# Attention into a Mish layer: tile 0's q as f32 on SyncE's queue, cast by three engines, and w_in issued ahead of v's casts

## The chip, the cores and the metric

The kernel runs on one core of one Trainium2 chip. The metric is the device time of one execution in microseconds (us); a time quoted for a kernel is the median of several runs. A core has five engines with a queue of instructions each: TensorE (PE, with its weight loads PEld), VectorE (DVE), ScalarE (ACT), GpSimd (POOL) and SyncE (SP). Each runs its queue in order and waits on semaphores for the others. Transfers (DMA) are issued from an engine's queue and move their bytes on 16 DMA engines.

## The reference

```
scores = q @ k^T / sqrt(64)                      # 8 batches, 8 heads, 576 positions, 64 wide
D[h]   = gamma_h ** (i - j) for i >= j, else 0   # gamma_h = 1 - 2 ** (-5 - h)
att    = (scores * D) @ v
x      = att, heads side by side                 # 4608 x 512
h      = x @ w_in                                # 512 x 2048
g      = h * tanh(softplus(h))                   # Mish
out    = g @ w_out                               # 2048 x 512
```

All inputs and the output are f32; the kernel multiplies in bf16.

## The kernel before

**Tiles.** The 4608 rows are cut into 36 chunks of 128 rows, and four chunks make a tile of 512 rows, so there are nine tiles. Tiles 0 and 1 hold the first 128 positions of each of the eight batches; they need no state of earlier positions and have a path of their own (functions whose names begin with `f_`). The other tiles carry a state matrix from chunk to chunk.

**The first layer** is `g1(t, f)` (L360): for one of 16 blocks `f` of 128 columns of w_in, four matmuls into `hp` and a Mish on ScalarE into `gT` (L367). For tile 0, blocks 0 to 3 are done in two halves of the columns, first for chunks 0 and 1 and then for chunks 2 and 3 (L456 to L461), blocks 4 to 15 whole (L487). The second layer follows with `g2_first`, `g2` and `g2_last`.

**The order of all work is written by hand** (`manual_schedule`): each engine runs its instructions in the order in which the program text names them. Waits come from the data.

**Tile 0's path.** `load_first_qk(t, i, b)` (L99) loads q (i = 0) or k (i = 1) of one batch, all heads, on GpSimd's queue; the transfer casts f32 to bf16 and its target is `stage`, the first of two buffers of `gT`. `load_first_v(b)` (L107) loads v of two batches as f32, also into `stage`. `f_transpose(t, g, i, parts)` (L175) transposes two batches (pair `g`) of q or k on TensorE and copies the result out of PSUM with the engines named in `parts`. `f_scores` (L198) makes the scores of a pair and multiplies them on VectorE by `dmask` (L208, two per pair). `f_v` (L213) casts v to bf16 with the engine that it is given, `f_out` (L218) multiplies scores and v and copies into `xT`, the input of `g1`. `keep_warm(n)` (L157) issues n matmuls on zeros, whose results are not used.

**GpSimd's queue at the start.** Loads of k and q of batches 0 and 1 (L117), `make_identity` for `ident` (needed by every transpose on TensorE, L125), `dist` (L126 to L130, from which VectorE makes `dmask` at L146), loads of k and q of batches 2 and 3 (L131), `pos`, v of batches 0 and 1, the first quarter of w_in (L139), v of batches 2 and 3. Then two casts of v (L447, L448), and only then the other three quarters of w_in (L449, L450), a third cast of v (L453), and the loads of tile 1 and w_out. The fourth cast of v is ScalarE's (L454), ahead of the first Mish in its queue. SyncE's queue issues the stores of the output and, late in the kernel, transposing transfers; it has nothing to issue in the first 50 us.

Of the kernel before, what the change touches and what calls it, by code (L numbers as in the profile page):

```python
# [10 lines left out]
F32 = mybir.dt.float32  # L11
BF16 = mybir.dt.bfloat16
AX = mybir.ActivationFunctionType
# [4 lines left out]
def kernel(  # L18
# [18 lines left out]
    nc = tc.nc  # L37
    B, H, S, D = q.shape
    assert (B, H, S, D) == (8, 8, 576, 64)
    P = 128  # L40
# [3 lines left out]
    nF = d_ff // P  # L44
    KC = d_model // P
    NCH = 4
# [15 lines left out]
    consts = ctx.enter_context(tc.tile_pool(name="consts", bufs=1))  # L62
# [6 lines left out]
    gp = ctx.enter_context(tc.tile_pool(name="gp", bufs=2))  # L69
    op = ctx.enter_context(tc.tile_pool(name="op", bufs=4))  # L70
    PS = bass.MemoryType.PSUM
    ps_sc = ctx.enter_context(tc.tile_pool(name="ps_sc", bufs=2, space=PS))
    ps_st = ctx.enter_context(tc.tile_pool(name="ps_st", bufs=1, space=PS))
# [11 lines left out]
    def load_w_in(f0, n):  # L85
        nc.gpsimd.dma_start(out=w_in_t[:, :, ds(f0, n)], in_=w_in_r[:, :, ds(f0, n)])
# [6 lines left out]


    stage = gp.tile([P, nF, NCH * P], BF16, name="gT")
    v0 = {}
    fst = {}

    def load_first_qk(t, i, b):  # L99

        name = ("qb", "kb")[i]
        if t not in fst:
            fst[t] = {"qb": stage[:, 0:4, :], "kb": stage[:, 4:8, :], "vb": {}}
        nc.gpsimd.dma_start(out=fst[t][name][:, b, :],  # L104
                            in_=(q, k)[i][4 * t + b, :, 0:P, :].rearrange("h (g r) d -> g h (r d)", r=8))

    def load_first_v(b):  # L107

        if b < 4:
            pair = stage[:, ds(8 + 2 * b, 4), :].bitcast(F32).rearrange("p a (c d) -> p (a c) d", d=D)  # L110
        else:
            pair = first.tile([P, 2 * H, D], F32, name="vpair", bufs=2)
        for e in range(2):
            v0[b + e] = pair[:, ds(H * e, H), :]
        nc.gpsimd.dma_start(out=pair, in_=v[ds(b, 2), :, 0:P, :].rearrange("b h p d -> p (b h) d"))

    for i, b in ((1, 0), (1, 1), (0, 0), (0, 1)):  # L117
        load_first_qk(0, i, b)

    zeros = consts.tile([P, 512], BF16)  # L120
    nc.vector.memset(zeros, 0.0)
    lnd = consts.tile([P, 1], F32)
    nc.vector.memset(lnd, -0.5 * math.log(D))
    ident = consts.tile([P, P], BF16)
    make_identity(nc, ident)  # L125
    dist = consts.tile([P, P], F32)  # L126
    nc.gpsimd.iota(dist, pattern=[[1, P]], base=0, channel_multiplier=-1,
                   allow_small_or_imprecise_dtypes=True)
    nc.gpsimd.affine_select(out=dist, in_=dist, compare_op=OP.is_ge, fill=1.0e6,
                            base=0, pattern=[[1, P]], channel_multiplier=-1)  # L130
    for i, b in ((1, 2), (1, 3), (0, 2), (0, 3)):  # L131
        load_first_qk(0, i, b)
    pos = consts.tile([P, 5], F32)
    nc.gpsimd.iota(pos, pattern=[[P, 5]], base=0, channel_multiplier=1,
                   allow_small_or_imprecise_dtypes=True)
# [2 lines left out]
    load_first_v(0)  # L138
    load_w_in(0, 512)  # L139
    load_first_v(2)  # L140
    mask = consts.tile([P, P], F32)
    mask2 = consts.tile([P, P], F32)
    lg = [math.log(1.0 - 2.0 ** (-5.0 - h)) for h in range(H)]
    dmask = consts.tile([P, H, P], F32)
# [12 lines left out]
    def keep_warm(n, pool=ps_o, name="ops"):  # L157
        idle = pool.tile([P, 512], F32, name=name)
        for _ in range(n):
            nc.tensor.matmul(idle, lhsT=zeros[:, 0:P], rhs=zeros, start=True, stop=True)  # L160
# [14 lines left out]
    def f_transpose(t, g, i, parts):  # L175

        name = ("qb", "kb")[i]
        out_t = first.tile([P, H, P], BF16, name=name + "T", bufs=2)
        n = 8 // len(parts)
        moves = []  # L180
        for j, (pool, tname, copy) in enumerate(parts):
            tp = pool.tile([P, 2, 8, P] if tname == "sc" else [P, 8, P], BF16, name=tname)
            tp = (tp[:, 0] if tname == "sc" else tp)[:, 0:n]
            for r in range(n):
                if t == 1:
                    mix = fst[1][name, "mix", g][:, n * j + r]
                    nc.tensor.transpose(tp[:, r, :], mix.rearrange("p x d -> p (x d)"), ident)
                else:
                    for x in range(2):
                        nc.tensor.transpose(tp[ds(64 * x, 64), r, :],  # L190
                                            fst[0][name][:, 2 * g + x, ts(n * j + r, D)], ident)
            moves.append((copy, out_t.rearrange("p h (g r) -> p h g r", r=8)[:, :, :, ds(n * j, n)],
                          tp.rearrange("p r (g h) -> p h g r", h=H)))
        for copy, to, src in moves:
            copy(to, src)
        fst[t][name, g] = out_t

    def f_scores(t, g, between=None):  # L198
        qT, kT = fst[t]["qb", g], fst[t]["kb", g]
        scs = [ps_sc.tile([P, 2, NP, P], F32, name="sc").rearrange("p a b i -> p (a b) i") for _ in range(2)]  # L200
        for h in range(H):
            for x in range(2):
                r = ds(64 * x, 64)
                nc.tensor.matmul(scs[x][:, h, :], lhsT=kT[r, h, :], rhs=qT[r, h, :], start=True, stop=True)  # L204
        for x in range(2):
            b = 2 * g + x
            sm = first.tile([P, H, P], BF16, name="sm0", bufs=4)
            nc.vector.tensor_tensor(sm, scs[x], dmask, op=OP.mult)  # L208
            fst[t]["sm", b] = sm
            if between and x == 0:  # L210
                between()

    def f_v(t, b, copy):  # L213
        vb = first.tile([P, H, D], BF16, name="vb", bufs=4)
        copy(vb, v0[4 * t + b])
        fst[t]["vb"][b] = vb

    def f_out(t, b, copy):  # L218
        if b == 0:
            xts[t] = xp.tile([P, KC, NCH * P], BF16, name="xT")  # L220
        vb = fst[t]["vb"][b]
        if t == 0:
            pool, name = ((ps_h, "hp"), (ps_h, "hp"), (ps_st, "st"), (ps_o, "ops"))[b]
            ot = pool.tile([P, NP, P], F32, name=name)
        else:
            ot = ps_sc.tile([P, 2, NP, P], F32, name="sc")[:, 0]
        for p in range(NP):
            for e in range(2):
                nc.tensor.matmul(ot[ds(64 * e, 64), p, :], lhsT=vb[:, 2 * p + e, :],
                                 rhs=fst[t]["sm", b][:, 2 * p + e, :],  # L230
                                 start=(p == 0), stop=True, skip_group_check=True)
        copy(xts[t][:, :, ts(b, P)], ot)
# [121 lines left out]
            xts[t] = xp.tile([P, KC, NCH * P], BF16, name="xT")  # L354
        nc.vector.tensor_copy(xts[t][:, :, ts(s, P)], ot)  # L355

    gts = {}
    outs = {}

    def g1(t, f, cols=slice(0, NCH * P)):  # L360
# [69 lines left out]
    dve, act, pool = nc.vector.tensor_copy, nc.scalar.copy, nc.gpsimd.tensor_copy  # L430


    half = (slice(0, 2 * P), slice(2 * P, 4 * P))
    keep_warm(7)
    f_transpose(0, 0, 1, [(ps_h, "hp", act), (ps_h, "hp", dve)])
    nc.scalar.activation(dmask, dmask, AX.Exp, bias=lnd[:, 0:1])
    f_transpose(0, 0, 0, [(ps_st, "st", act), (ps_o, "ops", dve)])
    for h in range(H):
        nc.vector.tensor_scalar(ex[:, :, h], pos, lg[h], None, op0=OP.mult)
    f_transpose(0, 1, 1, [(ps_h, "hp", act), (ps_h, "hp", act)])  # L440
    f_scores(0, 0)
    f_transpose(0, 1, 0, [(ps_st, "st", act), (ps_o, "ops", act)])
    keep_warm(4, ps_h, "hp")
    nc.scalar.activation(gq, ex, AX.Exp)
# [1 line left out]
    nc.scalar.activation(warm, lnd, AX.Mish)  # L446
    f_v(0, 0, pool)  # L447
    f_v(0, 1, pool)  # L448
    for i in range(1, 4):  # L449
        load_w_in(512 * i, 512)  # L450
    f_scores(0, 1, lambda: f_out(0, 0, dve))
    f_out(0, 1, act)
    f_v(0, 2, pool)  # L453
# [168 lines left out]
```

## Time and profile before

| | |
|---|---|
| runs | 317.28, 317.5, 318.41 us; median 317.5 |
| profiled execution | 319.16 us |
| its span, first to last instruction | 317.5 us |
| mean granted TensorE clock | 0.988 |
| TensorE busy | 302.5 us (95%) |
| VectorE, ScalarE, GpSimd busy | 133.2, 111.2, 144.7 us |
| GpSimd's transfer queue | 27.80 MB |
| the hardware queues (SyncE's and ScalarE's) | 14.03 MB |

The span is cut on the page into lists of instruction groups; a line of the timeline gives the start, the time taken, the engine, the line of the kernel, the operation, the tiles (written from read), and in brackets the idle time of the engine before it and what ended that. GB/s count bytes as they are written. A transfer that casts f32 to bf16 reads twice the bytes that it writes. The "granted clock" is TensorE's, as a share of full speed. A DMA share is a mean over the 16 DMA engines and can be over 1 where transfers overlap.

### The profile page before, as it was taken

The numbers are of one execution on the slowest core, as the hardware profiler recorded it, in microseconds if no ns is written. First come the engines' busy times: TensorE is split into PE (matmuls) and PEld (weight loads), VectorE is DVE, ScalarE is ACT, GpSimd is POOL, SyncE is SP. The second block draws the span as 40 slices with busy tenths as digits, with TensorE's granted clock in tenths as the row PEclk, the third lists the DMA queues.
The fourth block names the chain that finished last, engine by engine and source line by source line (L and its number), as shares of the span: only waits on it lengthen the run. The fifth ranks groups of instructions, "written<-read, shape, count | busy, mean of one in ns | idle before, by whom it ended". The sixth has DMA issues, their size and how long they took to land.

```text
span 317.5 us, 5784 instructions
## 1 busy us (share of the span) xinstructions
PE 302.5 (95%) x2423; PEld 153.7 (48%) x2462; DVE 133.2 (42%) x196; ACT 111.2 (35%) x184; POOL 144.7 (46%) x181
## 2 busy tenths in 40 slices
PE   6759999999999999999999799999999999999995
PEld 3435454555554554544444354545454544444444
DVE  2620357478645535453535453535354332001111
ACT  3536515754254533333333223232323232333300
POOL 8576866999893986456555326252010000000000
PEclk9779999999999999999999999999999999999999
DMA  6999999999993999999999999990414000110031
GB/s 95 201 185 200 203 224 195 282 190 169 224 206 92 145 156 203 167 152 171 153 140 75 228 95 207 133 168 33 96 42 99 33 35 33 36 33 33 35 99 66
DMA packets 73642, 42.33 MB, mean 133 GB/s; under 512 B 58640, under 2 KB 65040, under 8 KB 73616
## 3 DMA queue, kind: packets, MB, share of 16 engines
q0 software_dynamic: 49216, 27.80, 65.4%
q1 hardware_dynamic: 24256, 14.03, 24.8%
q8 instruction: 19, 0.31, 0.4%
q10 hardware_dynamic: 144, 0.13, 0.1%
q14 instruction: 7, 0.06, 0.1%
HBM read 38.80 MB, written 9.44 MB: 152 GB/s over the span
## 4 chain that ended last, share of the span: by engine, by line
PE 76%; DMA 16%; POOL 5%; issue 2%; ACT 0%; DVE 0%; POOLq 0%
PE hp L365 33%; PE ops L380 28%; DMA qkT<-qks 5%; PE hp L380 4%; DMA w_out_t<-in_moe_w_out_dram 4%; DMA qraw<-in_q_dram 4%; PE sc L294 2%; PE st L326 2%; DMA gT<-in_v_dram 2%; POOL gT L104 2%; DMA qks<-in_k_dram 2%; PE sc L346 2%; PE sc L351 2%; PE sc L281 1%; PE hp L408 1%
## 5 line engine op out<-in xcount | busy, mean ns | idle before, releaser
L365 PE MATMUL hp<-xT,w_in_t 128*128 128x512 bf16 (+1 forms) x562 | 142.2, 375 | 4.6 <-ACT gT L367 1.9
L367 ACT ACTIVATE gT<-hp 128x512 bf16<-128x512 f32 (+1 forms) x148 | 86.6, 586 | 158.1 <-PE hp L365 145.6
L380 PE MATMUL ops<-w_out_t,gT 128*128 128x512 bf16 x430 | 110.1, 379 | 0.4
L365 PEld LDWEIGHTS <-w_in_t 128*128 128x128 bf16 x592 | 55.4, 98 | 65.0 <-issue 2.7
L380 PEld LDWEIGHTS <-gT 128*128 128x128 bf16 x496 | 48.3, 98 | 58.1 <-issue 0.8
L416 DVE COPY res<-ops 128x512 f32<-128x512 f32 x28 | 19.3, 688 | 83.3 <-PE ops L380 79.6
L329 DVE TENSOR_TENSOR ssb<-st,diag 128x512 bf16<-128x512 f32 x32 | 21.9, 685 | 49.4 <-PE st L326 49.4
L256 POOL DMA_DIRECT2D qraw<-in_q_dram x24 | 22.1, 920 | 40.6 <-DVE qks L266 38.3
L272 POOL TENSOR_TENSOR vs<-vraw,gv 128x512 bf16<-128x512 f32 x28 | 30.0, 1080 | 20.2 <-issue 14.0
L298 DVE TENSOR_TENSOR sm<-sc,mask 128x1024 bf16<-128x1024 f32 x28 | 33.1, 1216 | 7.1 <-PE sc L294 6.9
L256 POOL DMA_DIRECT2D vraw<-in_v_dram x24 | 21.7, 904 | 1.5 <-DMA vpair<-in_v_dram 1.5
L256 POOL DMA_DIRECT2D qks<-in_k_dram x24 | 21.6, 901 | 1.4 <-DMA w_out_t<-in_moe_w_out_dram 0.8
L266 DVE TENSOR_TENSOR qks<-qraw,gq 128x512 bf16<-128x512 f32 x28 | 18.7, 702 | 0.0
L355 DVE CAST xT<-sc 128x512 bf16<-128x512 f32 x24 | 15.3, 681 | 0.0
L380 PE MATMUL hp<-w_out_t,gT 128*128 128x512 bf16 x61 | 14.7, 379 | 0.2
L282 ACT COPY qkT<-sc 128x1024 bf16<-128x1024 bf16 x10 | 10.1, 1010 | 8.0 <-PE sc L281 8.0
L260 POOL DMA_DIRECT2D qraw<-in_q_dram x8 | 5.6, 707 | 14.2 <-DVE qks L266 14.1
L208 DVE TENSOR_TENSOR sm<-sc,dmask 128x1024 bf16<-128x1024 f32 x8 | 9.5, 1220 | 6.1 <-PE sc L204 6.1
L294 PE MATMUL sc<-qkT 64*128 64x128 bf16 x224 | 9.2, 218 | 1.6 <-DMA qkT<-qks 1.6
L346 PE MATMUL sc<-qkT,ssb 128*64 128x128 bf16 (+1 forms) x224 | 9.5, 213 | 0.0
L294 PEld LDWEIGHTS <-qkT 64*128 64x128 bf16 x224 | 6.3, 94 | 6.6 <-issue 3.4
L351 PE MATMUL sc<-sm,vs 128*64 128x128 bf16 x192 | 9.4, 219 | 0.0
(98 smaller groups left out, 192.8 us busy)
## 6 DMA issues: line engine op xcount, KB each, us to landing
out_dram<-res SPq DMA_DIRECT2D x31, 256.0 KB, 4.3
qraw<-in_q_dram POOLq DMA_DIRECT2D x24, 256.0 KB, 5.7
vraw<-in_v_dram POOLq DMA_DIRECT2D x24, 256.0 KB, 8.2
qks<-in_k_dram POOLq DMA_DIRECT2D x24, 128.0 KB, 7.1
w_in_t<-in_moe_w_in_dram POOLq DMA_DIRECT2D x4, 512.0 KB, 9.0
w_out_t<-in_moe_w_out_dram POOLq DMA_DIRECT2D x4, 512.0 KB, 11.0
gT<-in_k_dram POOLq DMA_DIRECT2D x8, 128.0 KB, 6.2
gT<-in_q_dram POOLq DMA_DIRECT2D x8, 128.0 KB, 6.5
```

The lines of the kernel that those rows point to most:

```text
L256: nc.gpsimd.dma_start(out=t, in_=src[b, :, ds(P * c, P), :].rearrange("h p d -> p h d"))
L266: nc.vector.tensor_tensor(live[n]["qks"][:, 0], live[n]["q"], gq[:, c, :].unsqueeze(2).to_broadcast([P, H, D]), op=OP.mult)
L272: nc.gpsimd.tensor_tensor(vs, live[n]["v"], gv[:, c, :].unsqueeze(2).to_broadcast([P, H, D]), op=OP.mult)
L294: nc.tensor.matmul(sc[:, e, p, :], lhsT=qk[r, 1, p, :], rhs=qk[r, 0, p, :], start=True, stop=True)
L298: nc.vector.tensor_tensor(sm.rearrange("p e n i -> p (e n) i"), sc.rearrange("p e n i -> p (e n) i"), m.unsqueeze(1).to_broadcast([P, 2 * ...
L329: nc.vector.tensor_tensor(ssb.rearrange("p e n d -> p e (n d)"), st.rearrange("p n d -> p (n d)").unsqueeze(1).to_broadcast([P, 2, NP * 64 ...
L346: nc.tensor.matmul(ot[ds(64 * e, 64), p, ds(i0, iw)], lhsT=st_sb[bb, cc][:, e, p, :], rhs=qk[:, 0, p, ds(i0, iw)], start=(i0 == 0 and p == ...
L351: nc.tensor.matmul(ot[ds(64 * e, 64), p, :], lhsT=vs[:, 2 * p + e, :], rhs=sm[:, e, p, :], start=False, stop=True, skip_group_check=True)
L365: nc.tensor.matmul(hp[:, cols], lhsT=w_in_t[:, c, ts(f, P)], rhs=xts[t][:, c, cols], start=(c == 0), stop=(c == KC - 1))
L367: nc.scalar.activation(gts[t][:, f, cols], hp[:, cols], AX.Mish)
L380: nc.tensor.matmul(ops, lhsT=gts[t][:, f, ts(s, P)], rhs=w_out_t[:, f, :], start=(f == 0), stop=(f == nF - 1))
L416: copy(ot, ops)
```

## The change

q of tile 0 is now loaded as f32 on SyncE's queue, four transfers at the start. The target `q0` is the second half of the second `gT` buffer, which is `gts[0]`, where g1 of tile 0 writes its blocks 8 to 15 later. The casts to bf16, into the place in `stage` where the casting transfer wrote before, are four instructions: batches 0 and 1 on VectorE, batch 2 on ScalarE, batch 3 on GpSimd. k stays with GpSimd's queue. On that queue `dist` now comes ahead of `ident`, and the other three quarters of w_in are issued behind q's cast and ahead of v's casts. ScalarE's exponential of `dmask` moves ahead of the first transposes. `keep_warm` has one matmul more at the start, and two new calls of two and three matmuls stand around the first `f_scores`.

```diff
@@ -93,6 +93,8 @@
     stage = gp.tile([P, nF, NCH * P], BF16, name="gT")
+    gts = {0: gp.tile([P, nF, NCH * P], BF16, name="gT")}
+    q0 = gts[0][:, H:nF, :].bitcast(F32).rearrange("p (b a) c -> p b (a c)", a=2)
     v0 = {}
@@ -114,22 +116,24 @@
-    for i, b in ((1, 0), (1, 1), (0, 0), (0, 1)):
-        load_first_qk(0, i, b)
+    for b in range(4):
+        nc.sync.dma_start(out=q0[:, b, :], in_=q[b, :, 0:P, :].rearrange("h (g r) d -> g h (r d)", r=8))
+    for b in range(2):
+        load_first_qk(0, 1, b)
...
-    ident = consts.tile([P, P], BF16)
-    make_identity(nc, ident)
     dist = consts.tile([P, P], F32)
     nc.gpsimd.iota(dist, pattern=[[1, P]], base=0, channel_multiplier=-1,
                    allow_small_or_imprecise_dtypes=True)
     nc.gpsimd.affine_select(out=dist, in_=dist, compare_op=OP.is_ge, fill=1.0e6,
                             base=0, pattern=[[1, P]], channel_multiplier=-1)
-    for i, b in ((1, 2), (1, 3), (0, 2), (0, 3)):
-        load_first_qk(0, i, b)
+    ident = consts.tile([P, P], BF16)
+    make_identity(nc, ident)
+    for b in (2, 3):
+        load_first_qk(0, 1, b)
...
     load_first_v(2)
+    nc.gpsimd.tensor_copy(fst[0]["qb"][:, 3, :], q0[:, 3, :])
+    for i in range(1, 4):
+        load_w_in(512 * i, 512)
...
-    gts = {}
     outs = {}
...
-    keep_warm(7)
+    nc.scalar.activation(dmask, dmask, AX.Exp, bias=lnd[:, 0:1])
+    for b in range(2):
+        dve(fst[0]["qb"][:, b, :], q0[:, b, :])
+    keep_warm(8)
     f_transpose(0, 0, 1, [(ps_h, "hp", act), (ps_h, "hp", dve)])
-    nc.scalar.activation(dmask, dmask, AX.Exp, bias=lnd[:, 0:1])
     f_transpose(0, 0, 0, [(ps_st, "st", act), (ps_o, "ops", dve)])
     for h in range(H):
         nc.vector.tensor_scalar(ex[:, :, h], pos, lg[h], None, op0=OP.mult)
+    act(fst[0]["qb"][:, 2, :], q0[:, 2, :])
     f_transpose(0, 1, 1, [(ps_h, "hp", act), (ps_h, "hp", act)])
+    keep_warm(2, ps_sc, "sc")
     f_scores(0, 0)
+    keep_warm(3, ps_st, "st")
     f_transpose(0, 1, 0, [(ps_st, "st", act), (ps_o, "ops", act)])
...
     f_v(0, 1, pool)
-    for i in range(1, 4):
-        load_w_in(512 * i, 512)
     f_scores(0, 1, lambda: f_out(0, 0, dve))
```

## The prediction

> **What bounds the kernel now.** I read the page first, then the timeline of TensorE, then the table of one-microsecond stretches, and last the issues with their time to landing.
>
> The page says that TensorE is the engine to watch, and the timeline says where it is not yet busy.
>
> ```profile
> PE 302.5 (95%) x2423; PEld 153.7 (48%) x2462; DVE 133.2 (42%) x196; ACT 111.2 (35%) x184; POOL 144.7 (46%) x181
> ```
>
> ```profile
> 5.00 1.06 PE L190 MATMUL hp<-ident,gT 128*64 128x128 bf16 x15 [0.31 <-DMA gT<-in_k_dram]
> 7.42 0.41 PE L190 MATMUL st<-ident,gT 128*64 128x128 bf16 x7 [0.47 <-DMA gT<-in_q_dram]
> 9.23 0.85 PE L190 MATMUL hp<-ident,gT 128*64 128x128 bf16 x15 [0.92 <-DMA gT<-in_k_dram]
> 10.01 1.04 PE L204 MATMUL sc<-qbT,kbT 64*128 64x128 bf16 x16
> ...
> 14.81 0.97 PE L229 MATMUL hp<-sm,vb 128*64 128x128 bf16 x16 [0.64 <-POOL vb L215]
> 17.06 1.05 PE L365 MATMUL hp<-xT,w_in_t 128*128 128x256 bf16 x8 [0.53 <-DMA w_in_t<-in_moe_w_in_dram]
> 20.02 1.86 PE L365 MATMUL hp<-xT,w_in_t 128*128 128x256 bf16 x8 [1.91 <-ACT gT L367]
> 21.81 0.64 PE L229 MATMUL st<-sm,vb 128*64 128x128 bf16 x8
> 23.67 12.67 PE L365 MATMUL hp<-xT,w_in_t 128*128 128x256 bf16 x63 [0.79 <-DVE xT L232]
> ```
>
> From 23.67 on TensorE runs without a wait worth naming (39.58 of 40 us from 60 to 100, 99.36 of 100 from 200 to 300). So the end of the kernel is the start of that dense stretch plus a fixed amount of work. Whatever brings 23.67 forward shortens the kernel by the same, as long as operands keep up.
>
> What sets 23.67? Behind the 1.91 us wait at 20.02 stands ScalarE, which is in order and has the cast of tile 0's last v in front of its Mish:
>
> ```profile
> 19.07 0.62 ACT L215 CAST vb<-gT 128x512 bf16<-128x512 f32 x1 [2.66 <-DMA gT<-in_v_dram]
> 19.59 0.65 ACT L367 ACTIVATE gT<-hp 128x256 bf16<-128x256 f32 x2
> ```
>
> So the second pair of v (issued at 9.58, landed 9.5 us later) is the wait that ends last; w_in's first quarter (issued 8.81, 8.2 us to landing, 17.06) is the one before it. Neither is bound by its issue: both lie in GpSimd's queue behind eight q/k loads and v's first pair.
>
> ```profile
> w_in_t<-in_moe_w_in_dram POOLq DMA_DIRECT2D x1, 512.0 KB, 8.2
> gT<-in_v_dram POOLq DMA_DIRECT2D x1, 512.0 KB, 9.5
> ```
>
> The stretches show how full the transfers are (the last three columns are granted clock, DMA share, GB/s written):
>
> ```profile
> 2.00:3.00 1.00, 1.00 (x4) 0.35 (x3) 0.00 (x0) 0.09 (x1) 1.00 (x3) 1.00 0.28 18
> 4.00:5.00 1.00, 0.69 (x3) 0.13 (x1) 0.20 (x2) 0.00 (x0) 0.93 (x4) 1.00 1.04 142
> 17.00:18.00 1.00, 0.94 (x8) 0.80 (x9) 0.13 (x1) 0.00 (x0) 0.50 (x1) 1.00 0.63 107
> 20.00:21.00 1.00, 0.98 (x5) 0.69 (x5) 0.00 (x0) 0.24 (x1) 1.00 (x3) 0.50 1.19 192
> ```
>
> Nothing moves until about 2.7 us; then q and k come at about 140 GB/s written as bf16, 280 read as f32; there is a hole at 17. From 19.75 to about 23.15 the granted clock is half, so the second half of the first Mish block and two f_out run slowly.
>
> **The change, part by part.** *q on SyncE's queue.* Four q loads leave GpSimd's queue and go out on SyncE's, idle until 51.85. An issue there takes 0.33 us (the last store's row), so all four are out by about 0.8 + 4 x 0.33 = 2.1 us. The last half store lands 1.7 us after its issue, so bytes should flow from about 1.8 instead of 2.7: a head start of 0.9 us. The eight loads together read 2.1 MB; summing the stretches, their bytes are through at about 10.0, so they took 7.3 us, 287 GB/s. How fast a half of them goes as f32 on a second queue no row of before shows. Above: w_in, in larger pieces, is written at about 200 GB/s, 395 read, in 2.65 us a quarter; the whole 2.1 MB at that rate takes 5.3 us, 2.0 less. Below: v's first pair, the f32-to-f32 row, moved 0.52 MB in about 2.4 us, 218 GB/s; q's 1.05 MB at that rate is 4.8 us, with k's 3.65 in series 8.45, 1.15 more. The change in the landing of v's second pair is thus between 0.9 + 2.0 = 2.9 us earlier and 0.25 us later. I take 1.9 us earlier: q has the same 2 KB rows as w_in (v's are 256 B), so it is nearer to the upper end, and two queues can cover each other's ends of a load. That is 17.2 for v's second pair, 15.2 for w_in, 12.1 for v's first.
>
> The Trainium skill's page "DMA: Bandwidth & Descriptors", section "Issuing engines are not separate DMA queues", speaks against that rate: all queues run on the same 16 engines, and issuing from several saves only the issue. By it the head start alone would remain, v's second pair at 18.2 and 316.6 us.
>
> *GpSimd's queue.* It loses four issues (0.51 to 0.58 each, 2.2 us), and dist goes ahead of ident. k0 and k1 keep their place; dist is ready at about 3.2 instead of 4.77, ident at 3.9 instead of 4.19; k2 and k3 are issued from 3.9 instead of 4.72, v from 5.9 (7.61), w_in at 7.1 (8.81), v's second at 7.9 (9.58). Then one cast of q, 0.61 us (the row of vb's cast), at about 9.1; q3 should be there by 7. If it were not, w_in's other quarters and v's casts would wait behind it; they have some 3 us before v's first pair lands.
>
> *w_in's other quarters* (three issues, 2.24 us) move from 15.26 to about 9.7. They go past v's casts only, so the order of the transfers in the queue stays the same. This closes the hole at 17: 0.37 us of DMA. The quarters are used from about 25.4, 29 and 32 and landed at about 23.3, 26.4 and 28.4, so in themselves they are worth nothing; the hole's 0.37 us is kept as slack. An issue on this queue waits for the landing of the one eight places before it (at 44.13 k's load, for w_out's last quarter): eight before w_in's third and fourth quarters stand k0 and k1, landed by 6, so no wait comes in.
>
> *Casts of q.* Two on VectorE, one on ScalarE. Rows: 0.68 (xT's cast, from PSUM), 0.62 (vb on ScalarE); below, 0.41 for twice the elements in bf16 (kbx). So 0.2 to 0.7 each on VectorE, 1.4 at most. VectorE's dmask now ends at about 4.5 instead of 5.98, so the casts end by 5.9, before k's transposes (k1 lands at about 5.8 instead of 5.0, since it shares the engines with q). They hide behind k: nothing. ScalarE's dmask exp (1.15) goes ahead of the first copy, 4.5 to 5.65: hidden by the same wait; and if k1 landed at 5.0 as before, it would hold the first copy up by 0.1.
>
> *Attention's chain.* k's transposes end at 6.7, q's at 7.5 (8.06 before). k3 lands at about 8.4 (9.23), its transposes end at 9.1, two keep_warm take 0.43, scores start at 9.5 (10.01). VectorE's two masks of 1.2 us set the next scores, as before at +3.46: 13.0. xT's first column follows at about 15.5 (15.99). That is under w_in plus its slack: w_in's landing at 15.2 lets the first block start at 15.5 instead of 17.06.
>
> *keep_warm.* Six more of 0.22 to 0.43 us, 1.3 to 2.6 us on TensorE, all before 11 us, where it waits for k or for VectorE's masks: nothing, unless k comes early.
>
> *The sum.* v's second pair 1.9 earlier moves ScalarE's cast to 17.2, the first Mish to 17.7, TensorE's second half block to 18.1, and the dense start by 1.9, if the half-clock stretch lies over the same work. If it falls elsewhere, up to 1.3 us come on top (block 1.7 instead of 0.86, f_out 1.07 instead of 0.6). In before the clock changes at about 9.5, 12.9, 19.75 and 23.15, steps of 3.4 us or multiples; with the work 1.9 us earlier most of it would be over before 19.75, but a half-clock stretch over dense work then costs up to 1.7 itself. I add 0.4. Gain 2.3 us.
>
> Operands behind that: w_out's first quarter lands about 33.5 and is used at 37.07; the mix of tile 1's q ends at 33.4 and is used at 36.17. Both have 2.8 us or more and come forward with the queue: nothing.
>
> The profiled execution took 319.16 us, 1.66 around its span of 317.5; the median of the runs shown is 317.5. The gain comes off either alike: 315.2 from the median.
>
> **Rivals.** *Head start only.* One slow transfer engine sets every landing: summed bytes of v's second pair are through at 17.35, yet it lands at 19.07. If that engine gets no faster, the gain is 0.9, with 0.4 of clock 1.3: 316.2 to 317.3, within 0.5%. For it: 0.63 at 17 with v still outstanding. Against: q leaves that queue.
>
> *Both queues at full rate and the clock kept.* 2.9 earlier and 1.3 of clock: 313.3. For it: w_in's 395 GB/s. Against: k's loads are as small as before.
>
> *The other side: w_in's quarters crowd v out.* They are now queued right behind v's second pair. If the transfers mix instead of going one after the other, v's landing is put off by a quarter's 2.65 us or more, up to 7.9 for three. It decides from a landing later than 19.07; one quarter against the 0.9 of head start gives +1.75, 319.2. For it: the landing trails the summed bytes by 1.7 us. Against: in before each landing follows the order of issue.
>
> **How the numbers follow.** My forecast (gain 1.6 to 3.3, 314.2 to 315.9) gets 0.45, full rate and clock 0.16, head start or less 0.27, crowding 0.12. About 0.5%, 1.6 us, is what a measurement of this kernel can tell from no change. So faster 0.61, same 0.27, slower 0.12. The range runs from full rate, 313.3, to no change with 0.2 of spread, 317.7, and leaves the crowding out.
>
> **What would show it.** q's issues on SyncE at 0.8 with landings before 7; k1 no later than 6.5; v's second pair near 17.2; the dense stretch from about 21.4; the same TensorE work after it. Wrong if v's second pair lands after 18.5, if scores start after 10.5, or if waits for w_in or w_out appear after 21.

## The result and the profile after

The changed kernel takes 315.8 us (median of 16 runs) beside 318.2 us for the kernel before in the same comparison. The ratio is 0.9936, with a 95% interval of 0.9907 to 0.9965: 2.0 us faster (0.0064 x 318.2), between 1.1 and 3.0 us by the interval. Forecast were 315.2 us and a gain of 2.3. The size is about right; the way there was not the one that was forecast.

Executions of one kernel lie up to 8 us apart here, and a profile shows a single one: those of the changed kernel (317.75 us) and of experiments 1, 5, 7 and 9 are among the longest of their kernel.

The profiled execution has a span of 316.0 us (317.5 before). First the timeline of TensorE in the changed kernel, from the wait for k to the start of the dense stretch ("..." marks lines left out).

```profile
4.94 0.31 PE L197 MATMUL hp<-ident,gT 128*64 128x128 bf16 x1
7.19 0.63 PE L197 MATMUL hp<-ident,gT 128*64 128x128 bf16 x15 [1.94 <-DMA gT<-in_k_dram]
...
9.82 1.06 PE L197 MATMUL hp<-ident,gT 128*64 128x128 bf16 x15 [0.41 <-DMA gT<-in_k_dram]
11.21 0.63 PE L167 MATMUL sc<-zeros 128*128 128x512 bf16 x1 [0.33 <-issue]
11.78 1.13 PE L211 MATMUL sc<-qbT,kbT 64*128 64x128 bf16 x16
12.84 1.46 PE L167 MATMUL st<-zeros 128*128 128x512 bf16 x3
...
16.33 0.62 PE L211 MATMUL sc<-qbT,kbT 64*128 64x128 bf16 x16
...
18.95 2.10 PE L371 MATMUL hp<-xT,w_in_t 128*128 128x256 bf16 x16 [0.68 <-ACT vb L222]
...
22.41 3.82 PE L371 MATMUL hp<-xT,w_in_t 128*128 128x256 bf16 x22 [0.79 <-DVE xT L239]
```

The dense stretch starts at 22.41 instead of 23.67. The four half blocks of w_in now run through without a break (16 matmuls from 18.95), where they were torn apart by the wait for Mish, that is for v. But they start at 18.95, later than the 17.06 of before, since the first scores come at 11.78 instead of 10.01. Two things on TensorE's queue make these 1.77 us. k's fourth load, the last one that stands ahead of the scores, lands at 9.82 instead of 9.23: 0.6 us. And the two new warm matmuls (`sc<-zeros`; the trace has a record of one) stand between the transposes and the scores, where before nothing did: 1.1 us, at the half clock. k's second load is late too, at 7.19 instead of 5.00, a wait of 1.94 us; it does not hold the scores up by itself, for TensorE is idle again from 8.27 to 9.09, ahead of k's third load; but the half clock follows it. The second scores come 4.55 us after the first, not 3.46: VectorE waits 1.68 us for them (below), while TensorE works from 11.21 to 17 without a gap worth naming, three more warm matmuls at the half clock included.

The other engines' lines of the same timeline show that v is early now:

```profile
0.81 2.62 SPq L120 DMA_DIRECT2D gT<-in_q_dram  x4
11.94 1.18 POOL L222 CAST vb<-gT 128x512 bf16<-128x512 f32 x2 [0.37 <-DMA gT<-in_v_dram]
16.43 0.62 POOL L222 CAST vb<-gT 128x512 bf16<-128x512 f32 x1 [3.31 <-DMA gT<-in_v_dram]
16.98 1.23 DVE L215 TENSOR_TENSOR sm<-sc,dmask 128x1024 bf16<-128x1024 f32 x1 [1.68 <-PE sc L211]
18.12 0.68 DVE L239 CAST xT<-hp 128x512 bf16<-128x512 f32 x1
18.25 0.62 ACT L222 CAST vb<-gT 128x512 bf16<-128x512 f32 x1
```

v's second pair is there at 16.43, 2.64 us earlier than 19.07; GpSimd still waits for it. ScalarE doesn't any more: its cast at 18.25 has no wait in front, it is late because ScalarE was still busy with attention. The bound has passed from v's transfer to attention's own chain.

The stretches of one microsecond of the changed kernel (last three columns: granted clock, DMA share, GB/s written) show both sides of that:

```profile
2.00:3.00 1.00, 1.00 (x4) 0.36 (x3) 0.00 (x0) 0.09 (x1) 0.88 (x3) 1.00 0.64 131
4.00:5.00 1.00, 0.92 (x4) 0.07 (x1) 0.85 (x9) 0.37 (x1) 1.00 (x3) 1.00 1.12 295
9.00:10.00 1.00, 0.50 (x5) 0.31 (x7) 1.00 (x9) 0.23 (x1) 1.00 (x2) 0.50 1.06 258
14.00:15.00 1.00, 0.94 (x14) 0.77 (x15) 1.00 (x2) 0.00 (x0) 0.00 (x0) 0.50 1.14 242
17.00:18.00 1.00, 0.84 (x18) 0.56 (x17) 1.00 (x1) 0.99 (x3) 1.00 (x3) 1.00 1.22 203
```

The bytes start at about 2.3 instead of 2.7 (131 GB/s against 18 from 2 to 3), and the hole at 17 is closed. Where v's bytes are can be read from the packets in the kept traces, since v's are the only ones of 4096 bytes in the first 20 us. The first one starts at 8.42 instead of 9.76, the last one of the second pair ends at 15.63 instead of 18.32, and the landing follows 0.80 us later (0.75 before). So 1.34 us of the 2.64 are gained ahead of v's first byte, 1.35 us between its first and last. On the other side the granted clock is half from 8.6 to 15.4, all over attention's chain.

**One rule carries all that follows.** Span = start of the dense stretch + 292.1 us + what TensorE waits later. Before: 23.67 + 292.1 + 1.6 (one wait for a transposing transfer, qkT) = 317.4. Changed: 22.41 + 292.1 + 1.5 = 316.0. Experiments 2, 3, 4, 6, 10, 11 and 12 keep it within 0.4 us. It lacks a term where the clock falls to half over the dense stretch itself: 1.4 us are left over in experiment 8, 1.7 and 1.6 in 5 and 7 (3.4 us at half clock each, at about 130 us), 1.9 in 9; in 1 it is 0.7, with no such fall. So each experiment can be read by its dense start, if the clock behind it is looked at too.

### The profile page after: what moved, and what is told of

It is laid out like the page before. It is cut to its first block, busy times and chain, and to the rows that moved or that the text cites. A ratio compares the mean times of both kernels' runs of the same rounds, so it can differ in the third digit from the quotient of the medians.

```text
span 316.0 us, 5807 instructions
## 1 busy us (share of the span) xinstructions
PE 302.7 (96%) x2428; PEld 153.4 (49%) x2468; DVE 135.3 (43%) x198; ACT 111.7 (35%) x185; POOL 143.0 (45%) x178
## 4 chain that ended last, share of the span: by engine, by line
PE 74%; DMA 20%; POOL 3%; issue 1%; ACT 0%; DVE 0%; POOLq 0%
PE hp L371 31%; PE ops L386 26%; DMA qkT<-qks 9%; PE hp L386 4%; DMA w_out_t<-in_moe_w_out_dram 4%; DMA qraw<-in_q_dram 4%; PE sc L301 2%; DMA vraw<-in_v_dram 2%; PE st L333 2%; DMA gT<-in_k_dram 2%; PE sc L353 1%; PE sc L358 1%; PE sc L288 1%; PE hp L414 1%; POOL gT L106 1%
## 5 line engine op out<-in xcount | busy, mean ns | idle before, releaser
L422 DVE COPY res<-ops 128x512 f32<-128x512 f32 x28 | 19.3, 688 | 83.4 <-PE ops L386 79.6
L273 DVE TENSOR_TENSOR qks<-qraw,gq 128x512 bf16<-128x512 f32 x28 | 19.9, 746 | 0.0
```

Of the source, the lines that this page charges most:

```text
L273: nc.vector.tensor_tensor(live[n]["qks"][:, 0], live[n]["q"], gq[:, c, :].unsqueeze(2).to_broadcast([P, H, D]), op=OP.mult)
L422: copy(ot, ops)
```

## The experiments

The theory after the result: q on a second queue brings v 2.6 us forward; most of this is lost again since q's bytes crowd k's first loads, and since the wait for k costs TensorE's full clock. Rivals: the place of w_in's quarters makes the gain; k is late for another reason; the clock does not matter. Two more have no run: the changed kernel without its two new calls of warm matmuls, and the kernel before with fifteen warm matmuls at the start.

**1. w_in's place alone, on the kernel before.**

```diff
     load_first_v(2)
+    for i in range(1, 4):
+        load_w_in(512 * i, 512)
...
     f_v(0, 1, pool)
-    for i in range(1, 4):
-        load_w_in(512 * i, 512)
```

> The kernel before with one part of the change alone: the other three quarters of w_in issued ahead of v's casts. Theory (q's second queue brings v earlier; the place of w_in brings only the hole at 17): v's second pair lands at 18.7 to 19.1, the dense stretch starts at 23.3 to 23.7, time within 0.4 us of before. Rival (w_in's place brings the gain): dense start near 22.4, 1.3 us faster. Rival (w_in's quarters crowd v): v's second pair later than 19.5, slower by 0.5 or more.

TensorE's timeline of this kernel:

```profile
16.92 1.05 PE L367 MATMUL hp<-xT,w_in_t 128*128 128x256 bf16 x8 [0.91 <-DMA w_in_t<-in_moe_w_in_dram]
19.98 1.87 PE L367 MATMUL hp<-xT,w_in_t 128*128 128x256 bf16 x8 [2.01 <-ACT gT L369]
...
23.63 2.53 PE L367 MATMUL hp<-xT,w_in_t 128*128 128x256 bf16 x17 [0.79 <-DVE xT L234]
```

23.63 for 23.67; v's second pair at 19.03 for 19.07. Ratio to the kernel before 1.0037 (0.9997 to 1.0077). The place of w_in gains nothing, and its quarters do not crowd v: the prediction's rival on the slower side falls here.

**2. The same part undone, in the changed kernel.**

```diff
     nc.gpsimd.tensor_copy(fst[0]["qb"][:, 3, :], q0[:, 3, :])
-    for i in range(1, 4):
-        load_w_in(512 * i, 512)
...
     f_v(0, 1, pool)
+    for i in range(1, 4):
+        load_w_in(512 * i, 512)
```

> The changed kernel with that one part undone: w_in's quarters issued behind two of v's casts again. Theory: v's first pair is there at about 12 and the quarters go out at about 13 instead of 9.3, dense start 22.3 to 22.7 as in the changed kernel, time the same within 0.4 us; the quarters still land before their use. Rival (w_in's place brings the gain): dense start near 23.5, 1.2 us slower than the changed kernel.

Its timelines, GpSimd and TensorE:

```profile
13.18 2.24 POOL L86 DMA_DIRECT2D w_in_t<-in_moe_w_in_dram  x3
...
22.18 4.04 PE L369 MATMUL hp<-xT,w_in_t 128*128 128x256 bf16 x23 [0.79 <-DVE xT L237]
```

The quarters go out at 13.18 instead of 9.34, and the dense stretch starts at 22.18, as with the whole change. Ratio 0.9944 (0.9914 to 0.9975). From both sides: all of the gain belongs to q's move and what goes with it (the order of `dist`, `ident` and the exponential, and the warm matmuls, which no run separates from it).

**3. Fifteen warm matmuls instead of eight.**

```diff
-    keep_warm(8)
+    keep_warm(15)
     f_transpose(0, 0, 1, [(ps_h, "hp", act), (ps_h, "hp", dve)])
```

> The changed kernel with keep_warm(15) in place of 8 ahead of the first transposes, so that TensorE works on zeros until about 6.5 to 7.5 while k is on its way. Theory (the changed kernel loses to the half clock from 8.8 to 15.2 that follows its wait for k): the granted clock stays full from 8 to 12, first scores at about 11.2 instead of 11.8, second scores at about 15 instead of 16.3, dense start 21.2 to 21.8, 0.6 to 1.2 us faster than the changed kernel. Rival (the landing of k alone sets the chain): the clock is kept and the dense start stays at 22.2 to 22.5. Third case: the clock falls all the same, and nothing moves.

TensorE's timeline:

```profile
3.37 3.39 PE L167 MATMUL ops<-zeros 128*128 128x512 bf16 x10
6.69 0.24 PE L197 MATMUL hp<-ident,gT 128*64 128x128 bf16 x1
7.41 0.63 PE L197 MATMUL hp<-ident,gT 128*64 128x128 bf16 x15 [0.47 <-DMA gT<-in_k_dram]
...
10.85 0.73 PE L211 MATMUL sc<-qbT,kbT 64*128 64x128 bf16 x16
...
13.97 0.70 PE L211 MATMUL sc<-qbT,kbT 64*128 64x128 bf16 x16
...
16.64 2.10 PE L371 MATMUL hp<-xT,w_in_t 128*128 128x256 bf16 x16 [0.65 <-DVE xT L239]
...
20.10 6.20 PE L371 MATMUL hp<-xT,w_in_t 128*128 128x256 bf16 x33 [0.79 <-DVE xT L239]
```

k is no earlier (7.41), yet the first scores come 0.9 us earlier, the second 2.4, and the dense stretch starts at 20.10, 2.3 us earlier than in the changed kernel; the granted clock is full in every stretch, and fifteen of the transposes at 9.75 take 0.63 us where the changed kernel's take 1.06 at 9.82. That is more than the 0.6 to 1.2 that was expected. Ratio to the kernel before 0.9897 (0.9845 to 0.9949), an interval that overlaps that of the change itself. The changed kernel's profile is one with a fallen clock (mean 0.989); seven of its sixteen executions have this mean, and their median span is 314.4 us, that of the other nine 313.5. So over all executions seven idle-looking matmuls are worth less than the 2.3 us of this pair of profiles: the medians are 0.7 to 1.8 us apart (315.8 for the change; 314.0, 314.5, 314.55 and 315.13 in experiments 3, 10, 11 and 12, measured beside the kernel before at 317.31 to 318.66).

**4. q held back until k's first loads are issued.**

```diff
-    for b in range(4):
-        nc.sync.dma_start(out=q0[:, b, :], in_=q[b, :, 0:P, :].rearrange("h (g r) d -> g h (r d)", r=8))
     for b in range(2):
         load_first_qk(0, 1, b)
+    for b in range(4):
+        nc.gpsimd.memset(q0[0:1, b, 0:1], 0.0)
+    for b in range(4):
+        nc.sync.dma_start(out=q0[:, b, :], in_=q[b, :, 0:P, :].rearrange("h (g r) d -> g h (r d)", r=8))
```

> The changed kernel with q's four loads on SyncE held back until k's first two loads are issued on GpSimd's queue (a one-element write of GpSimd into q's place, which q's loads must follow). Theory (q's bytes crowd k's first two loads, which land at 4.9 and 7.2 instead of 4.3 and 5.0): k's second lands at 5.0 to 5.5, first transposes of k end at 6.2, and v's second pair lands 0.7 to 1.2 later than in the changed kernel (17.1 to 17.6). First scores no later than 10.5, dense start 20.8 to 22. Rival (k is late for another reason, GpSimd's queue or the memory): k's second still lands at 7, and all else is as in the changed kernel or later by the delay of q.

TensorE's timeline:

```profile
4.78 1.31 PE L199 MATMUL hp<-ident,gT 128*64 128x128 bf16 x16
8.70 0.96 PE L199 MATMUL st<-ident,gT 128*64 128x128 bf16 x8 [2.61 <-DVE gT L444]
...
11.29 1.06 PE L199 MATMUL hp<-ident,gT 128*64 128x128 bf16 x15 [1.19 <-DMA gT<-in_k_dram]
...
13.24 1.13 PE L213 MATMUL sc<-qbT,kbT 64*128 64x128 bf16 x16
...
24.03 2.12 PE L373 MATMUL hp<-xT,w_in_t 128*128 128x256 bf16 x16 [0.79 <-DVE xT L241]
```

All of k's first sixteen transposes run through from 4.78, the second of them at 5.03: without q beside it, k's second load is there by then, as it was at 5.00 before. So q's bytes do crowd k by some 2.2 us. The rest of the expectation missed. q, issued from 2.65, is now the late one (TensorE waits 2.61 us for its cast), k's fourth load comes at 11.29, v's second pair at 18.84 (expected 17.1 to 17.6). The dense stretch starts at 24.03, and the ratio is 1.0035 (1.0000 to 1.0071). What k gained, q and everything behind it lost; and of v's 2.64 us only 0.23 are left when q's loads start 1.84 us later.

**5. The half clock by itself, on the kernel before.**

```diff
     for f in range(4):
         g1(0, f, half[0])
+        if f == 1:
+            keep_warm(8)
```

> The kernel before with keep_warm(8) put between the second and the third block of the first half of the first layer of tile 0, where TensorE waited from 18.1 to 20.0 for ScalarE's Mish. Nothing of the change is in it. Theory (the half clock over that work is worth 1.3 us, a term of the prediction's sum): the granted clock stays full from 17 to 24, v's second pair still lands at 19.0, the third block starts at 20.0 to 20.2 and the dense stretch at 22.3 to 22.7 instead of 23.67; 0.8 to 1.4 us faster than before. Rival (the clock falls all the same, or falls later over dense work): dense start 23.5 or more, or half clock behind it, and no gain.

TensorE's timeline:

```profile
17.48 1.89 PE L160 MATMUL ops<-zeros 128*128 128x512 bf16 x7
20.38 1.03 PE L365 MATMUL hp<-xT,w_in_t 128*128 128x256 bf16 x8 [1.00 <-ACT gT L367]
...
22.77 3.60 PE L365 MATMUL hp<-xT,w_in_t 128*128 128x256 bf16 x22 [0.79 <-DVE xT L232]
...
128.11 0.40 PE L294 MATMUL sc<-qkT 64*128 64x128 bf16 x8 [2.19 <-DMA qkT<-qks]
```

The third and fourth half blocks took 1.86 us before and take 1.03; from their start to the dense stretch it is 2.39 us instead of 3.65. The term of 1.3 us in the prediction is confirmed as 1.26. v's second pair was 0.36 later in this execution (19.43), so the dense start is 22.77, 0.9 before the old one. The timed runs show nothing of it: 1.0002 (0.9961 to 1.0043), an interval that just about takes in 0.9 us (0.28%). The last line, a wait of 2.19 us at 128 with half the clock after it, stands in one long execution (320.55 us) and cannot explain that; why the timed runs gain nothing stays open.

**6. q's transposes ahead of k's.**

```diff
+    f_transpose(0, 0, 0, [(ps_st, "st", act), (ps_o, "ops", dve)])
     f_transpose(0, 0, 1, [(ps_h, "hp", act), (ps_h, "hp", dve)])
-    f_transpose(0, 0, 0, [(ps_st, "st", act), (ps_o, "ops", dve)])
```

> The changed kernel with TensorE's transposes of q's first pair ahead of k's. q is cast by 6.6, k's second load lands at 7.2. Theory (k's landing sets the chain, and TensorE's wait for it then costs the clock): q's transposes fill part of the wait, k's end at 7.9 instead of 8.3, first scores up to 0.4 us earlier; whether the clock is kept from 8.8 depends on whether 0.9 us of transposes before 7.2 counts as work. If kept, dense start 20.5 to 21.5; if not, 21.9 to 22.4. Rival (order on TensorE is nothing): as the changed kernel, 22.4.

TensorE's timeline:

```profile
6.83 0.64 PE L197 MATMUL st<-ident,gT 128*64 128x128 bf16 x7 [1.16 <-DVE gT L442]
...
7.58 1.17 PE L197 MATMUL hp<-ident,gT 128*64 128x128 bf16 x16
...
9.66 1.06 PE L197 MATMUL hp<-ident,gT 128*64 128x128 bf16 x15 [0.30 <-DMA gT<-in_k_dram]
...
11.63 1.13 PE L211 MATMUL sc<-qbT,kbT 64*128 64x128 bf16 x16
...
21.23 5.12 PE L371 MATMUL hp<-xT,w_in_t 128*128 128x256 bf16 x28 [0.79 <-DVE xT L239]
```

First scores at 11.63, only 0.15 earlier, but the dense start is 21.23: in the range expected for a kept clock. Yet it was not kept so: fifteen transposes at 9.66 take 1.06 us, as in the cold, against 0.63 in experiment 3. Here TensorE had never come to full speed; it did at about 12.7, while the changed kernel's execution fell to half at 8.6 and came back at 15.4. Ratio 0.9918 (0.9886 to 0.9951), not to be told from the change itself. What the order on TensorE is worth, this profile cannot separate from where the clock changed.

**7. Half of q back on GpSimd's queue** (13 warm matmuls; batches 2 and 3 of q as casting loads behind k, their two casts left out as they are not needed).

```diff
-    for b in range(4):
+    for b in range(2):
         nc.sync.dma_start(out=q0[:, b, :], in_=q[b, :, 0:P, :].rearrange("h (g r) d -> g h (r d)", r=8))
...
-    for b in (2, 3):
-        load_first_qk(0, 1, b)
+    for i, b in ((1, 2), (1, 3), (0, 2), (0, 3)):
+        load_first_qk(0, i, b)
```

> The kernel with 15 warm matmuls changed again: only q of batches 0 and 1 goes as f32 on SyncE's queue; q of batches 2 and 3 is loaded by casting transfers on GpSimd's queue behind k, as before, and has no casts on engines; 13 warm matmuls. Theory (q's bytes crowd k): with half of them gone from the first 5 us, k's second lands at 5.8 to 6.4 instead of 7.2 to 7.4, first scores at 9.3 to 10.3 instead of 10.85; v's second pair lands at 16.5 to 17.6, so the dense start is 19.5 to 20.8, the same as with all four on SyncE within 0.7 us. Rival (only the number of queues matters, not the bytes): k's second at 7.2 as before the edit, and v's second pair a microsecond later.

TensorE's timeline:

```profile
6.60 0.63 PE L196 MATMUL hp<-ident,gT 128*64 128x128 bf16 x15 [0.41 <-DMA gT<-in_k_dram]
...
9.12 0.73 PE L210 MATMUL sc<-qbT,kbT 64*128 64x128 bf16 x16
...
18.83 1.03 PE L370 MATMUL hp<-xT,w_in_t 128*128 128x256 bf16 x8 [1.98 <-ACT gT L372]
...
21.22 5.12 PE L370 MATMUL hp<-xT,w_in_t 128*128 128x256 bf16 x28 [0.79 <-DVE xT L238]
```

k's second load is 0.8 us earlier than with all of q beside it (6.60), first scores 1.7 us earlier (9.12). But v's second pair lands at 17.88, between the 16.4 of all four and the 19.07 of none, and v is the bound again (1.98 us behind ScalarE's cast). So the two halves of q bring v forward by 1.2 and 1.4 us in these profiles, and k pays. The landings alone would not carry this, since with all of q moved they lie between 16.36 and 18.05 in eight profiles. The packets do: all but the last three of v's are through at 17.5 to 18.0 us with none of q moved (before, 1, 5), at 16.7 with half, and at 15.5 to 16.0 in those eight (the changed kernel, 2, 3, 6, 8, 10, 11, 12). Dense start 21.22, above the 19.5 to 20.8 expected; ratio 0.9972 (0.9929 to 1.0014).

**8. First scores ahead of the transposes of k's second pair** (15 warm matmuls).

```diff
-    f_transpose(0, 1, 1, [(ps_h, "hp", act), (ps_h, "hp", act)])
     keep_warm(2, ps_sc, "sc")
     f_scores(0, 0)
     keep_warm(3, ps_st, "st")
+    f_transpose(0, 1, 1, [(ps_h, "hp", act), (ps_h, "hp", act)])
     f_transpose(0, 1, 0, [(ps_st, "st", act), (ps_o, "ops", act)])
```

> The changed kernel with 15 warm matmuls, and TensorE's first scores ahead of the transposes of k's second pair, which wait for k's later loads until 9.75. Theory (attention's chain, through VectorE's two masks of 1.2 us, sets the dense start now, no longer v): first scores at 9.2 to 9.6 instead of 10.85, second scores at 12.5 to 13.2 instead of 13.97, first block of w_in at 15.0 to 15.6 instead of 16.64, and then v's second pair at 16.45 is the bound again: dense start 19.2 to 19.7 instead of 20.1, 0.4 to 0.9 us faster. Rival (v's landing is already the bound): dense start stays at 20.1.

TensorE's timeline:

```profile
9.85 0.62 PE L211 MATMUL sc<-qbT,kbT 64*128 64x128 bf16 x16 [0.49 <-ACT gT L448]
...
13.71 0.62 PE L211 MATMUL sc<-qbT,kbT 64*128 64x128 bf16 x16 [0.44 <-ACT qbT L202]
...
19.01 1.66 PE L371 MATMUL hp<-xT,w_in_t 128*128 128x256 bf16 x8 [1.65 <-ACT gT L373]
...
22.45 3.89 PE L371 MATMUL hp<-xT,w_in_t 128*128 128x256 bf16 x17 [0.79 <-DVE xT L239]
```

A miss. The first scores come a microsecond earlier, but the second only 0.26, for ScalarE now has four copies in a row in front of them. And in this execution v's second pair landed at 18.05 instead of 16.4, which brought the wait for Mish back, and with it the half clock from 19.3 on, over the dense stretch itself: span 315.9 = 22.45 + 292.1 + 1.35. Ratio 0.9917 (0.9878 to 0.9956). It does not beat experiment 3, and it shows that a landing of v can vary by 1.6 us between two kernels whose loads are the same. In the trace a single packet makes the difference: it ends at 17.16, all the others of v by 15.81.

**9 to 12. The late waits.** The runs of the kernel before lie 4.8 us apart (315.78 to 320.58), those of the changed one 3.8 (314.12 to 317.89), of experiment 2 1.7 (314.50 to 316.20); experiments 1, 5 and 7 have 5.7 to 7.8. Profiles with long waits for qkT between 120 and 195 us (1.6 before, 1.5 in the changed kernel, 3.2, 2.2 and 2.7 in experiments 1, 5 and 7) belong to the wide ones, those with none to the narrow ones (2, 3, 6). All of the narrow ones have the whole of q off GpSimd's queue. This is weak evidence: the profiles with long waits are also those of long executions, one for each kernel, and experiment 8 has no such wait, the whole of q off the queue, and runs 4.0 us apart. Experiments 9, 10 and 12 ask which side of that move matters; 11 repeats experiment 3.

Experiment 9, on the kernel before:

```diff
+    spare = consts.tile([P, 4, D], F32)
+    for b in range(4):
+        nc.sync.dma_start(out=spare[:, b, :], in_=q[b, 0, 0:P, :])
     for i, b in ((1, 0), (1, 1), (0, 0), (0, 1)):
         load_first_qk(0, i, b)
```

> The kernel before with four spare loads of 32 KB (128 pieces each, like q's loads, but 256 B long) on SyncE's queue at the start; nothing reads them, and GpSimd's queue is as before. It asks why kernels with all of q on SyncE's queue also vary less from run to run and rarely wait for a transposing transfer late in the kernel. Theory S (four more transfers on SyncE's queue ahead of its later stores and transposes): waits for qkT under 0.3 us, runs within 3 us of each other, median about 316.3. Theory G (four fewer issues on GpSimd's queue) and theory T (the time at which the dense stretch starts): runs spread over 5 us as before, median 317 to 318. Dense start 23.5 to 24 in each case.

Measured: runs 316.26 to 321.48, so 5.2 us apart; ratio 0.9962 (0.9921 to 1.0004). Four more transfers on SyncE's queue do not remove the spread, and the profile waits 0.6 us for qkT. With the spare loads, small as they are, the early landings of this execution were late: w_in's first quarter came at 18.72 and the dense stretch at 25.23, outside the expected 23.5 to 24, and the clock was half from 19.8 to 30.0.

Experiment 10, on experiment 3:

```diff
-        nc.sync.dma_start(out=q0[:, b, :], in_=q[b, :, 0:P, :].rearrange("h (g r) d -> g h (r d)", r=8))
+        nc.scalar.dma_start(out=q0[:, b, :], in_=q[b, :, 0:P, :].rearrange("h (g r) d -> g h (r d)", r=8))
```

> The changed kernel with 15 warm matmuls and q's four loads issued on ScalarE's queue in place of SyncE's. Dense start 20 to 20.8 (ScalarE's issues take 2.6 us there, ahead of its first copies). Theory S (four more on SyncE's queue is what keeps the late waits away): late waits for qkT come back, runs spread over 4 us or more, median 315 to 316. Theory G (four fewer issues on GpSimd's queue) or T (an early dense start): runs within 2 us of each other, median 313.8 to 314.8.

Measured: runs 314.15 to 315.19, median 314.5, ratio 0.9864 (0.9809 to 0.9918), dense start 20.83, no wait for qkT. The queue from which q is issued need not be SyncE's, so together with experiment 9 theory S falls.

Experiment 11, the edit of experiment 3 again:

> The changed kernel with 15 warm matmuls once more, for a narrower interval. Dense start 20.1, median 314.0, 1.0% (0.7 to 1.3%) under before. If its four earlier runs were lucky, the median is 315 or more.

Measured: median 314.55 (314.25 to 316.47), ratio 0.9875 (0.9827 to 0.9922), dense start 20.75, 0.65 later than expected (k's fourth load lands at 10.40, where it was 9.75). The gain of experiment 3 holds; the median is 0.55 us over the expected one.

Experiment 12, on experiment 3:

```diff
     f_v(0, 1, pool)
+    spare = consts.tile([P, 4, D], BF16)
+    for b in range(4):
+        nc.gpsimd.dma_start(out=spare[:, b, :], in_=q[b, 0, 0:P, :])
```

> The changed kernel with 15 warm matmuls and four spare casting loads put on GpSimd's queue in its idle time between v's second and third cast (128 pieces each, nothing reads them), so that this queue has as many issues in all as in the kernel before. Theory G (the number of issues on GpSimd's queue decides whether the transposing transfers late in the kernel are slow): dense start 20 to 21 as without them, but late waits for qkT come back, runs spread over 4 us or more, median 315.5 to 317. If not G: runs within 2 us, median 314 to 315; the number of issues is not it, and the cause of the late waits stays open.

GpSimd's and TensorE's timelines of experiment 12:

```profile
13.00 2.13 POOL L462 DMA_DIRECT2D spare<-in_q_dram  x4
...
19.97 6.19 PE L371 MATMUL hp<-xT,w_in_t 128*128 128x256 bf16 x34 [0.79 <-DVE xT L239]
```

Measured: runs 314.21 to 316.71, median 315.13, ratio 0.9941 (0.9902 to 0.9980), and no wait for qkT in its profile. The waits did not come back, which speaks against the number of issues on GpSimd's queue; but the spread of 2.5 us and the median lie between what the two theories expected, and the profile is one execution. An early dense start alone does not explain it: experiment 7 starts at 21.22 and has a wait of 2.67, experiment 4 starts at 24.03 and has one of 0.17. Why the transposing transfers wait less often stays open.

## Why the prediction was right, and where it was wrong

*The bound of before* was read rightly: the dense start sets the end, and v's second pair set the dense start. The rule of 292.1 us holds from 19.97 (experiment 12: 292.1 + 1.2 of later waits) to 24.03 (experiment 4), where the clock stays full behind it. The prediction's other sentence on this, that a half clock over dense work costs up to 1.7 us itself, is borne out by experiments 5 and 7 (1.7 and 1.6).

*q on SyncE's queue.* The head start was mis-sized: 0.44 us for 0.9, since the first bytes come at 2.29, 1.5 us after the first issue. An issue takes 0.65 us there (2.62 for four), not 0.33. The landing of v's second pair was forecast 1.9 us earlier between 2.9 and -0.25, and measured 2.64. The prediction summed bytes as if they moved in the order of issue, and found that the landing trails them by 1.7 us; v's own packets end only 0.75 us ahead of it, so most of that trail was bytes of v still moving. In before the last six packets of v end one after the other from 17.79 to 18.32, in the changed kernel all between 15.57 and 15.63. That one slow transfer engine had less to do once q left GpSimd's queue would fit; this is argued, not shown.

The Trainium skill's page "DMA: Bandwidth & Descriptors", section "Issuing engines are not separate DMA queues", has that several issuing engines save only the issue. The prediction took that as the head start alone, with v's second pair at 18.2; 16.43 is measured, and 16.36 to 18.05 in all eight profiles with all of q on a second queue from the start. The measurement decides: here the second queue was worth more than the 0.44 us of head start. How much of it is the queue itself stays open, since GpSimd's issues were saved with it (v's first pair is issued at 5.16 instead of 7.61), and in experiment 4, on the same second queue but started at 2.65, the landing is at 18.84.

*w_in's quarters*: nothing, as forecast, shown from both sides (1 and 2).

*Casts of q*: 0.43 and 0.57 us on VectorE, 0.63 on ScalarE, 0.61 on GpSimd, all behind the wait for k. As forecast; the last quarter of q landed at 8.78, not by 7, and its cast was still ahead of the 9.1 of the forecast.

*Attention's chain* is the step that failed, and with it *keep_warm*, a term put at nothing. The chain had k's second load at 5.8, its fourth at 8.4 and the first scores at 9.5; measured 7.2, 9.82 and 11.78. k shares the engines with q for longer than was worked out, and the wait for it was followed by the half clock. The new warm matmuls were to lie before 11 us, in waits; they lie on TensorE's queue between k's last transposes and the first scores (1.1 us, where the chain counts 0.43) and between the first scores and the second (1.46 us). The second scores were to come 3.46 us after the first, set by VectorE's masks; they came 4.55 after, set by TensorE at the half clock. First scores at 9.5 would, by the prediction's own sums, have left v the bound; at 11.78 attention became it, and the first block came at 18.95, not 15.5. The price of the half clock over this chain, warm matmuls included, is 1.6 to 2.4 us of dense start: 22.41 against 20.10, 20.83, 20.75 and 19.97 in experiments 3, 10, 11 and 12. What the chain would take without the new warm matmuls was not run. The prediction spoke of the half clock as a possible loss over dense work, and looked for it from 19.75 on, not over attention. It did write down scores after 10.5 as a mark of its being wrong, and that mark was hit.

*The sum.* Dense start forecast 21.4, measured 22.41: 1.26 us gained instead of 2.3. The timed gain of 2.0 is larger than the profile's 1.26; the changed kernel's profile is of one of its longest executions, with the fallen clock and 1.5 us of late waits. How much of the difference is the clock of the other executions and how much their late waits, no run separates; neither was in the prediction. So it was in part luck that the number came out near. *Both queues at full rate and the clock kept* was the rival with 313.3: experiments 3 and 11, at 0.9897 and 0.9875 of 317.5, are 314.2 and 313.5. With seven more warm matmuls the time comes near it, though v's landing is 2.64 us earlier, not 2.9.

## What to carry to other kernels

When a transfer is moved to a second queue, ask what it now travels beside, not only what it no longer travels behind: the q loads freed v and delayed k. A wait in front of TensorE can be priced twice, once as the wait and once as the half clock over whatever comes next; fill it with work that costs nothing, and with enough of it. Work on zeros costs nothing only inside a wait: between two steps of a chain each such matmul is 0.43 us at the half clock. Where a long dense stretch sets the end, read each variant by the start of that stretch, because that shows a microsecond in one profile that the timed runs may hide, and check that the clock stays full behind it.

## What the runs showed of the hardware

- Eight warm matmuls last 3.6 us, and did not always bring full speed: in the changed kernel's execution the transposes at 7.19 ran at 0.63 us for fifteen (0.63 at 6.99 in experiment 2), in experiment 6 at 1.06 us as late as 9.66, with the same eight in front. In experiment 4 TensorE works from 1.26 to 6.09 without a gap over 0.1 us, and its transposes at 11.29 still take 1.06. Fifteen of them, 5.5 to 6.1 us, were followed by transposes at full speed in all five profiles that have them (3, 8, 10, 11, 12). The Trainium skill's page "TensorE: Matmul & The Clock Gate", Part 1, says that the clock is judged in free-running windows of about 3.4 us. The traces agree: the half clock lasted 3.4 us twice in before (from 9.5 and from 19.75) and 6.8 us in the changed kernel (from 8.6). An estimate by the page's figure: work of 3.6 us covers a whole window in few of its positions, fifteen matmuls of 0.43 us, 6.4 us, in most.
- The granted clock reads 1.00 in a trace until its first change, also while matmuls take twice their time: the warm matmuls at the start have about 0.43 us each beside a clock of 1.00, and in experiment 6 it stays at 1.00 while transposes and scores run at half speed up to 12.7 us, where the trace has its first record of the clock. The duration of a known matmul is the better sign.
- v's second pair landed 0.7 to 0.9 us after the end of its own last packet in the profiles of before, the changed kernel and experiments 3, 7, 8 and 11, whether that came at 15.63 or at 18.32. A sum of all bytes in the order of issue gave 1.7 us for before: packets of several loads mix, and a single late one holds a landing back (experiment 8).
